# Attention and a capacity-routed mixture of experts on one core: five routing searches end after ten rounds, their count products get a later place, and the last 64 rows of an expert become one piece of the schedule

## The chip, the core and the metric

The kernel runs on one core of a Trainium2 chip. The metric is the time of the whole kernel on the device in microseconds (us), the median of several runs. TensorE (PE in the profile) multiplies matrices; PEld is its weight load. VectorE (DVE), ScalarE (ACT) and GpSimd (POOL) work on elements; SyncE (SP) starts transfers. Each engine takes its instructions strictly in the order in which the program lists them. An instruction that waits therefore holds everything behind it on its engine.

## The reference

Attention over 8 batches, 8 heads, 576 positions and 64 values, with a causal mask by blocks of 64, gives 4608 rows of 512 values. Each row goes to exactly one of 8 experts, and each expert takes exactly 576 rows:

```python
logits = x @ w_gate                       # 4608 x 8
order = np.argsort(-logits.flatten())
for idx in order:                         # from the largest logit down
    tok, e = idx // E, idx % E
    if assigned[tok] >= 0 or counts[e] >= cap: continue
    assigned[tok] = e; counts[e] += 1     # cap = 576
for e in range(E):
    mask = assigned == e
    out[mask] = np.maximum(x[mask] @ w1[e], 0) @ w2[e]   # 512 -> 1024 -> 512
```

Which expert fills first, and with which rows, depends on the data, so the kernel has to find it out on the chip.

## The kernel before

**Attention** takes the first half of the span and is not touched. It leaves the rows in DRAM (`x`) and the logits on the chip (`L`).

**The expert part** fills experts one after another. Step k (0 to 7) finds the expert that fills next, its 576 rows, and then computes them. `route(k)` is the search. Each row that is still free proposes to its best remaining expert (L740, L756, L758), and for all 8 experts at once the kernel looks for the value above which exactly 576 proposals lie. It does so in rounds. A round divides the interval in four: three candidates are written (L795, VectorE), two of them are counted on VectorE (L803, `jk`), the third on ScalarE (L772, `ja`, a sum of signs), a small product on TensorE adds the counts over the partitions (L819, `tot`, the count product), and VectorE turns the totals into the next step (L822, `sg`). After round t the interval is 4 to the power of minus t in the units of the search, so 14 rounds (`NS=14`) resolve the numbers fully. In round 6 (`NSC=6`) ScalarE also writes a shifted copy of the proposals (L776), with which the later, finer rounds work. `finish` (L898) then takes the highest threshold of the 8 experts (`heads`, L825), `place` and `invert` turn the rows found into a list of indices with three groups of small products (L963 to L967, `po`; L1065, `pe`; L1072, `ps`), and POOL gathers the rows by that list (L1140).

Step 0 and step 1 are different. Step 0 has four rounds and a guess that it checks. Step 1 has eight rounds (`EX={1:8}`) and then `early` (L874): one more pass on VectorE counts the proposals below the threshold found so far (L879), a product adds them up (L883, `wn`), and three short operations (L887 to L890) form a flag that is non-zero only when a single expert has the highest threshold and exactly 576 proposals lie above it. VectorE loads the flag into a register and branches (L892 to L896): where the flag is zero, `general` (L849) runs the rounds that were left out, on VectorE alone; otherwise it is skipped. Step 7 needs no search, since one expert is left.

`ffn(k)` computes an expert's 576 rows. The first product (L1191, `h`) has two halves of 256 and 320 rows with eight groups of 12 matmuls each; each group is taken out of its PSUM bank by ScalarE (L1177, `HH`) and VectorE (L1179, `HL`). Four banks carry the tag `g`. The second product (`y`) has five parts: m = 0 to 3 with 128 rows (L1217, eight pieces of three matmuls), and m = 4 with the last 64 rows (L1221, four pieces of six matmuls, which use half the columns of the array at a time, in pairs). The weights of an expert come in 8 transfers (`raw`), which ScalarE splits in halves (L1102, L1106) and POOL subtracts (L1109). POOL may start on them only when the next search has begun (`began`, L700, and the gate of L1108), and there are six `raw` buffers.

**The order of the work** is written by a planner, `Sched`, when the program is built. Each task is a Python generator that yields the engine, the cost in ns and the events that it needs, and then emits the instructions of one piece. The planner keeps a planned time for each engine and picks the task that can start first, a task of a better priority (lower number) before others; the order that comes out is fixed in the program. A search has priority 0, its count product too; `ffn` has priority 3. `lag(t)` moves the planned readiness of a task's next piece back by t ns. It emits nothing: it only changes where the planner puts the piece among those of its engine. The next search (k) is let in when the second product of expert k-2 begins (event `mid`). Planned costs that matter here are 645 ns for a piece of L1217 and 720 ns for a piece of L1221.

## Time and profile before

| what | us |
| --- | --- |
| median of three runs | 772.76 (770.9 to 775.21) |
| the profiled execution's own time | 774.55 |
| its span (first to last instruction) | 772.1 |
| PE busy | 712.9 (92%) |
| DVE busy | 554.8 (72%) |
| ACT busy | 533.0 (69%) |
| POOL busy | 467.2 (61%) |

The profile is one execution. Its time lies 2.45 us above its span, and 1.79 us above the median of the runs. Rows of the timeline read: start, duration, engine, line and operation, what it writes and reads, shapes, count; in brackets how long the engine was idle before it, and what ended the wait. Steps are told apart by time: the second products of experts 1, 2, 3 and 4 begin near 444, 495, 546 and 597 us, and the searches for experts 3, 4, 5 and 6 with them.

### The profile page before, as it was taken

To read this page: it belongs to the slowest core of one execution; us is meant where nothing else is said; L and a number is where in the kernel's file an instruction comes from. 1 tells how busy PE (TensorE), PEld (TensorE's weight loads), DVE (VectorE), ACT (ScalarE), POOL (GpSimd) and SP (SyncE) were. 2 spreads that over 40 slices of the span, in tenths; PEclk is the share of its full clock that TensorE was granted. 3 is DMA by queue.
4 is the path that set the end of the run, shared out by engine and by line. 5 is a ranking of instruction groups with operands and counts; after the bars stand their busy time and mean duration, and the time that the engine had idled before them with its cause. 6 is when DMAs were issued, how large, how long until landed. Compare 5 with 4: busy or idle time off the path is not lost.

```text
span 772.1 us, 18932 instructions
## 1 busy us (share of the span) xinstructions
PE 712.9 (92%) x6493; PEld 473.3 (61%) x6493; DVE 554.8 (72%) x2260; ACT 533.0 (69%) x1438; POOL 467.2 (61%) x520
## 2 busy tenths in 40 slices
PE   5889999999999999966999989999999999999997
PEld 3556676766776777743545736547557475574753
DVE  6899889998799878768897968579587693420210
ACT  5788888988898898844755696774865848383211
POOL 5888878997799876613431485480762825766001
PEclk9999999999999999987999999999999999999999
DMA  9888999999999994256267291933915719862101
GB/s 203 164 157 171 204 188 213 205 166 226 191 203 179 215 211 85 78 124 209 81 183 214 91 284 37 276 107 100 260 65 207 162 38 268 276 164 62 35 14 48
DMA packets 249122, 122.83 MB, mean 159 GB/s; under 512 B 205600, under 2 KB 232096, under 8 KB 249024
## 3 DMA queue, kind: packets, MB, share of 16 engines
q1 hardware_dynamic: 243088, 102.60, 59.7%
q0 software_dynamic: 5936, 19.01, 7.5%
q8 instruction: 51, 0.84, 0.4%
q14 instruction: 47, 0.39, 0.2%
HBM read 71.45 MB, written 18.87 MB: 117 GB/s over the span
## 4 chain that ended last, share of the span: by engine, by line
PE 37%; DVE 5%; ACT 4%; DMA 4%; issue 2%; POOL 1%; another core or an unknown queue 0%; POOLq 0%; SPq 0%; DVEq 0%; ACTq 0%
PE y L1217 18%; PE h L1191 16%; PE y L1221 2%; DMA out_dram<-yo,ix 2%; ACT W L1106 1%; ACT raw L1102 1%; DMA raw<-in_moe_w_dram 1%; DVE jk L803 1%; DVE HL L1179 1%; POOL xg L1140 1%; DVE cd L795 1%; DMA xg<-x,ix 1%; PE pe L1065 1%; ACT ja L772 0%; ACT HH L1177 0%
## 5 line engine op out<-in xcount | busy, mean ns | idle before, releaser
L442 POOL TENSOR_TENSOR P<-P,m 128x320 f32<-128x320 f32 (+8 forms) x285 | 209.4, 771 | 45.9 <-DVE m L434 30.6
L1191 PE MATMUL h<-X,W 128*128 128x320 f16 (+3 forms) x1536 | 194.9, 286 | 1.0 <-DVE HL L1179 0.5
L1191 PEld LDWEIGHTS <-W 128*128 128x128 f16 x1536 | 142.5, 98 | 45.5 <-issue 4.8
L420 ACT ACTIVATE P<-psb,m 128x576 f32<-128x576 f32 (+8 forms) x288 | 149.7, 548 | 25.6 <-DVE m L413 17.8
L1217 PE MATMUL y<-W,HH 128*128 128x512 f16 x512 | 152.2, 379 | 0.0
L409 DVE TENSOR_REDUCE m<-psb 128x1 f32<-128x576 f32 (+8 forms) x288 | 124.7, 479 | 10.8 <-PE psb L384 10.5
L1109 POOL TENSOR_TENSOR W<-raw,W 128x1024 f16<-128x1024 f32 x56 | 118.1, 2135 | 14.4 <-ACT W L1106 12.8
L467 PE MATMUL psb<-mident,P 128*128 128x128 f32 x800 | 104.5, 278 | 11.1 <-POOL P L442 5.1
L384 PEld LDWEIGHTS <-qT 128*64 128x64 f16 x1408 | 77.1, 111 | 42.3 <-issue 28.1
L1177 ACT ACTIVATE HH<-h 128x320 f16<-128x320 f32 (+3 forms) x128 | 51.8, 409 | 71.6 <-PE h L1191 64.0
L1207 POOL DMA_INDIRECT out_dram<-yo,ix x40 | 39.0, 975 | 102.6 <-ACT yo L1199 65.5
L384 PE MATMUL psb<-kT,qT 128*64 128x288 f16 (+8 forms) x704 | 90.8, 284 | 10.8 <-ACT P L420 9.6
L467 PEld LDWEIGHTS psb<-mident,P 128*128 128x128 f32 x800 | 86.3, 141 | 22.6 <-POOL P L442 7.0
L1140 POOL DMA_INDIRECT xg<-x,ix x40 | 40.9, 1023 | 96.5 <-DVE ix L1074 51.5
L502 PE MATMUL psb<-PT,V 128*64 128x448 f32 (+5 forms) x776 | 97.2, 388 | 0.9 <-DVE PT L450 0.4
L1179 DVE SCALAR_TENSOR_TENSOR HL<-h,HH 128x320 f16<-128x320 f32 (+3 forms) x128 | 57.2, 452 | 55.8 <-ACT HH L1177 47.7
L1217 PE MATMUL y<-W,HL 128*128 128x512 f16 x256 | 97.0, 379 | 0.0
L448 ACT ACTIVATE PT<-psb 128x512 f32<-128x512 f32 (+1 forms) x165 | 82.6, 596 | 6.0 <-PE psb L467 5.7
L384 PE MATMUL psb<-kS,qT 128*64 128x288 f16 (+8 forms) x704 | 83.2, 281 | 0.4 <-DVE kS L354 0.2
L1217 PEld LDWEIGHTS <-HH 128*128 128x128 f16 x512 | 46.9, 97 | 50.2 <-issue 0.4
L1102 ACT ACTIVATE raw<-raw 128x512 f32<-128x512 f32 x112 | 67.9, 625 | 8.4 <-DMA raw<-in_moe_w_dram 8.2
L502 PEld LDWEIGHTS psb<-PT,V 128*64 128x64 f32 x776 | 49.5, 137 | 32.2 <-issue 24.3
(251 smaller groups left out, 1018.5 us busy)
## 6 DMA issues: line engine op xcount, KB each, us to landing
raw<-in_moe_w_dram SPq DMA_DIRECT2D x64, 512.0 KB
x<-XR SPq DMA_DIRECT2D x8, 1152.0 KB
kn<-in_k_dram SPq DMA_DIRECT2D x15, 576.0 KB
qn<-in_q_dram SPq DMA_DIRECT2D x15, 576.0 KB
V<-in_v_dram SPq DMA_DIRECT2D x64, 128.0 KB
V<-in_v_dram SPq DMA_DIRECT2D x16, 64.0 KB
xg<-x,ix POOLq DMA_INDIRECT x41
out_dram<-yo,ix POOLq DMA_INDIRECT x40
```

Source lines behind the costliest of these rows:

```text
L384: nc.tensor.matmul(out if len(K1.shape) == 2 else out.rearrange("p (r j) -> p r j", r=2), lhsT=A[:, h, 64 * i:64 * i + 64], rhs=K1, start= ...
L409: nc.vector.tensor_reduce(m[:, 0, c:c + 1], ps[:, o:o + 64 * (i + 1)] if g else s.part(ps, g, i, o), axis=AX.X if g else AX.XY, op=OP.max)
L420: nc.scalar.activation(out, in_, AF.Exp, bias=m[:, 1, c:c + 1], scale=s.ESC, accum_out=m[:, 2, c:c + 1])
L442: nc.gpsimd.tensor_tensor(sl, sl, m[:, 3, c:c + 1].to_broadcast([P, w]), op=OP.mult)
L448: s.nc.scalar.activation(out, in_, AF.Copy)
L467: nc.tensor.transpose(ps[:, a], s.Pb[n % s.NP][:, s.OFF[i] + 128 * j:s.OFF[i] + 128 * j + P], s.ident)
L502: nc.tensor.matmul(ps[64 * h:64 * h + 64, 64 * (i0 - b0):64 * (b1 - b0)], lhsT=vn[:, j, 2 * (n % 2) + h, :], rhs=pt[:, s.PTI[(j, i0)]:s.PT ...
L1102: nc.scalar.activation(raw[:,x],raw[:,x],AF.Copy,scale=s.WS)
L1109: nc.gpsimd.tensor_tensor(lw,raw,hi,op=OP.subtract)
L1179: nc.vector.scalar_tensor_tensor(HL[:,f,ts],ps,0.0,HH[:,f,ts],op0=OP.max,op1=OP.subtract)
L1191: nc.tensor.matmul(ps,lhsT=W[:,a,d,f*P:f*P+P],rhs=X[:,4*(d//2)+d%2+l,ts],start=(d==0 and n==0),stop=(d==3 and n==2))
L1217: if m<4: nc.tensor.matmul(ps,lhsT=Z[:,f,m*P:m*P+P],rhs=Y[:,a,f],start=(f==n==0),stop=(f==7 and n==2))
```

## The change

Three edits:

1. `EX` gets the steps 2 to 6 with ten rounds each. These searches now run rounds 0 to 9, leave out the shifted copy of round 6, and go through `early` with its extra pass, product, flag and branch. The body that is skipped holds four rounds.
2. After the passes of a round of a search k > 1 the planner is told to place the count product later: 800 ns in the first round, 300 ns in the others.
3. For k > 0 the part m = 4 of the second product is one piece of 2880 planned ns. The same 24 matmuls come out in the same order; the planner can no longer put another task between them.

```diff
-        s.NS=14; s.NSC=6; s.NX=4; s.EX={1:8}
+        s.NS=14; s.NSC=6; s.NX=4; s.EX={1:8,2:10,3:10,4:10,5:10,6:10}
...
                     if live: sc.busy(D,330 if k==0 else 150)
+                    if live and k>1: sc.lag(300 if t else 800)
                     yield T,30,('sg',k,t)
                     tot=s.ps.tile([P,512],F32,tag="tot",name=f"tot{k}_{t}")
                     nc.tensor.matmul(tot[:,0:3],lhsT=s.bo,rhs=cnt,start=True,stop=True)
...
             for f in range(8 if m<4 else 4):
-                yield T,645 if m<4 else 720,*[(x,k,y) for g in ((f,) if m<4 else (f,f+4)) for x,y in (('h',g),('h',8+g),('wc',4+g//2))],'g' if f==0 else None
+                wf=[(x,k,y) for g in ((f,) if m<4 else (f,f+4) if k==0 else range(8)) for x,y in (('h',g),('h',8+g),('wc',4+g//2))]
+                if m<4 or k==0 or f==0: yield T,645 if m<4 else 720 if k==0 else 2880,*wf,'g' if f==0 else None
                 if f==0: gk=sc.gtake(); ps=s.ps.tile([P,512],F32,tag="g",name=f"y{k}_{m}",bufs=4)
```

## The prediction

> **What bounds the kernel now.** I read the page first, then the busy time by stage of the expert part, then the waits, then the timeline around each wait of TensorE.

> ```profile
> PE 712.9 (92%) x6493; PEld 473.3 (61%) x6493; DVE 554.8 (72%) x2260; ACT 533.0 (69%) x1438; POOL 467.2 (61%) x520
> ...
> q8 instruction: 51, 0.84, 0.4%
> ```

> PE is busy for 92%, so shorter work elsewhere counts only where it lets PE stop waiting. The view of stages (start and end, length, busy time of PE, PEld, DVE, ACT, POOL) cut at the first matmul of experts 1 to 7 shows how much that is:

> ```profile
> 416.26:470.36 54.10, 50.06 (x381) 30.64 (x380) 43.12 (x230) 43.25 (x104) 34.49 (x24) 1.00 0.51 160
> 470.36:521.12 50.76, 49.55 (x378) 30.33 (x376) 38.14 (x206) 34.83 (x84) 28.17 (x20) 1.00 0.51 154
> 521.12:571.97 50.85, 49.63 (x379) 30.42 (x377) 38.20 (x206) 34.80 (x84) 26.55 (x19) 1.00 0.57 154
> 571.97:622.90 50.93, 49.54 (x379) 30.38 (x377) 38.09 (x206) 34.58 (x84) 26.55 (x19) 1.00 0.55 153
> 622.90:671.67 48.77, 48.77 (x370) 30.16 (x368) 28.29 (x108) 28.01 (x61) 26.78 (x19) 1.00 0.75 213
> 671.67:719.93 48.26, 48.26 (x358) 30.03 (x356) 8.28 (x19) 25.16 (x53) 27.32 (x19) 1.00 0.41 109
> ```

> Expert 6, beside which no search runs, takes 48.26 us without a gap, at a granted clock of 1.00. Experts 1 to 5 take 5.84, 2.50, 2.59, 2.67 and 0.51 us more: 14.1 us, the most that this change could return. Who stops PE from 416 to 672 us is said by its waits:

> ```profile
> PE tot L819 <- ACT ja L772: 5.1, 4, 1.4
> PE tot L819 <- DVE jk L803: 2.1, 1, 2.1
> PE po L964 <- DVE MM L920: 0.6, 1, 0.6
> ```

> Five count products hold PE for 7.2 us. Each is placed in PE's order at a point that PE reaches before the counts are there. One of the five, and what its neighbours do (PE, then ACT, then DVE), and the four others:

> ```profile
> 550.18 0.38 PE L1217 MATMUL y<-W,HL 128*128 128x512 f16 x1
> 551.77 0.16 PE L819 MATMUL tot<-cn,m_bo 128*128 128x3 f16 x1 [1.21 <-ACT ja L772]
> ...
> 554.16 0.38 PE L1217 MATMUL y<-W,HL 128*128 128x512 f16 x1
> 554.38 0.17 PE L819 MATMUL tot<-cn,m_bo 128*128 128x3 f16 x1
> 554.41 0.59 PE L1217 MATMUL y<-W,HH 128*128 128x512 f16 x2
> ```

> ```profile
> 548.38 0.44 ACT L1177 ACTIVATE HH<-h 128x320 f16<-128x320 f32 x1 [0.95 <-remote]
> ...
> 551.06 0.56 ACT L772 ACTIVATE ja<-m_PB,bs 128x324 f16<-128x324 f32 x1
> ```

> ```profile
> 551.55 0.08 DVE L803 DVE_READ_ACCUMULATOR jk<-m_PB,bs 128x1 f16 x1
> ```

> ```profile
> 419.64 0.16 PE L819 MATMUL tot<-cn,m_bo 128*128 128x3 f16 x1 [1.25 <-ACT ja L772]
> ...
> 454.21 0.18 PE L819 MATMUL tot<-cn,m_bo 128*128 128x3 f16 x1 [2.12 <-DVE jk L803]
> ...
> 501.00 0.16 PE L819 MATMUL tot<-cn,m_bo 128*128 128x3 f16 x1 [1.21 <-ACT ja L772]
> ...
> 602.79 0.16 PE L819 MATMUL tot<-cn,m_bo 128*128 128x3 f16 x1 [1.39 <-ACT ja L772]
> ```

> The rows at 501.00, 551.77 and 602.79 are the first rounds of the searches for experts 4, 5 and 6: ACT is late, because the weights' conversions fill its queue and one `HH` waited 0.95 us, so `ja`, and DVE's passes, end only near 551.6. The two at 419.64 and 454.21 lie inside the searches for experts 2 and 3.

> **The change part by part.**

> *Ten rounds and a test.* Four rounds go from each of five searches, so 20 count products leave PE's order. One costs PE 554.41 - 554.16 = 0.25 us against 0.215 for a matmul of L1217 (half of the 0.43 between neighbours): 0.035 us, so 0.7 us. What the test adds is seen once, in the search for expert 1:

> ```profile
> 381.19 0.51 DVE L879 TENSOR_SCALAR_CACHE_REDUCE jx<-m_PB,CB 128x288 f16<-128x288 f32 x1
> ...
> 385.16 0.17 DVE L890 SCALAR_TENSOR_TENSOR x<-wn,x 128x8 f32<-128x8 f32 x1
> ...
> 386.51 0.19 DVE L908 TENSOR_TENSOR sm<-m_BC,f 128x32 f32<-128x32 f32 x1 [1.17 <-DVEq L896]
> ```

> ```profile
> 382.23 0.17 PE L883 MATMUL wn<-m_bo,cx 128*128 128x8 f16 x1
> 382.26 7.54 PE L1191 MATMUL h<-X,W 128*128 128x448 f16 x39
> ```

> That is some 0.5 us of pass, 0.6 us of short operations (about three at 0.2 us) and 1.17 us in which DVE loads and branches: 2.3 us on DVE per search, against four rounds of about 2 us. Behind the branch on DVE stand the `HL` that free PSUM banks. In the row at 382.26 PE runs 39 matmuls without a gap through the whole of it, so it is covered; the product `wn` costs PE 0.035 us if its pass is ready, five times, and up to a DVE pass of 0.5 us each if not. I take 0.1 us each, 0.5 us, nearer the row.

> The search is not what the experts wait for, but it moves other work:

> ```profile
> 528.60 0.10 PEld L819 LDWEIGHTS <-m_bo 128*128 128x128 f16 x1 [0.28 <-DVE jk L803]
> ```

> ```profile
> 533.08 0.14 DVE L917 CAST eidx<-m 128x1 int32<-128x1 f32 x1
> ...
> 549.46 0.06 DVE L700 MEMSET gate<- 128x1 f32 x1
> ```

> ```profile
> 534.69 5.87 DMA raw<-in_moe_w_dram
> ```

> The search for expert 4 runs its 14 products from 501.00 to 528.60, 27.6/13 = 2.12 us a round. Ten end near 501.0 + 9 x 2.12 = 520.1, and with the m = 4 part in the way near 521; the test adds 2.3, so `eidx` comes at about 528.5 instead of 533.1. The weights' eight transfers on SP's queue and the five gathers on POOL's start some 4.5 us sooner. Both queues are free for it: X is needed only at 571.97. ACT can convert six pieces (six `raw` buffers; POOL frees none before the gate at 549.46), so its backlog before the first round of the next search should end some 4 us sooner too. That is a second reason for the stalls at 501, 551 and 602 to shrink, beside the lag.

> *The lag.* It adds no instruction. A piece of L1217 is 0.645 us (three matmuls). 800 ns puts one piece, or two, ahead of the first count product; what PE does in the wait is then work. So each of the three stalls (1.21, 1.21, 1.39 idle; 1.37, 1.37 and 1.55 us with the rest of the pitch, since 551.77 - 550.18 - 0.215 = 1.37) loses between 0 (ACT later by as much) and all. One piece alone would return 0.645; with the earlier conversions I take 1.2 each, 3.6 us. What becomes late is the first round, by no more than now, as PE waits for that product already. 300 ns in the other rounds is less than half a piece: a round of three pieces (1.94 us) mostly stays one. For the stalls at 419.64 and 454.21 (with the same 0.16 more, 1.41 and 2.28 us) the ends are 0 and the whole. The second has an odd cause:

> ```profile
> 452.54 0.16 DVE L822 SCALAR_TENSOR_TENSOR sg<-tot,m_wk 128x3 f32<-128x3 f32 x1 [2.65 <-PE y L1217]
> ```

> ```profile
> 449.96 0.17 PE L819 MATMUL tot<-cn,m_bo 128*128 128x3 f16 x1
> ```

> ```profile
> 450.16 0.92 POOL L1140 DMA_INDIRECT xg<-x,ix  x1 [0.30 <-issue]
> ```

> DVE got word of a product of 449.96 only at 452.5, while POOL was gathering. The gathers of expert 2 move ahead, so I take 1.3 of the 2.28; of the 1.41 I take 0.5. In the first product (h) the last products of a search wait a little (0.28 before the weight load at 528.60) and go with their rounds: 0.1 a search, 0.5 us in all, between 0 and 1.4.

> *The last 64 rows as one piece.* Today a count product falls inside L1221 in experts 1 to 4:

> ```profile
> 518.18 0.62 PE L1221 MATMUL y<-W,HH 128*64 128x512 f16 x4
> ...
> 520.25 0.18 PE L819 MATMUL tot<-cn,m_bo 128*128 128x3 f16 x1
> ...
> 521.12 1.16 PE L1191 MATMUL h<-X,W 128*128 128x256 f16 x9
> ```

> ```profile
> 668.96 0.62 PE L1221 MATMUL y<-W,HH 128*64 128x512 f16 x4
> ...
> 671.67 1.59 PE L1191 MATMUL h<-X,W 128*128 128x256 f16 x13
> ```

> 2.94 us with it, 2.71 without: 0.23 each, 0.9 us. Its cost is that a count product can wait 2.7 us behind the block, which the search can afford.

> *Sum:* 0.7 - 0.5 + 3.6 + 1.3 + 0.5 + 0.5 + 0.9 = 7.0 us. Against the profiled execution's 774.55 that gives 767.5; the median lies 1.8 lower, so **765.8 us**. The bounds: with no stall gone 0.7 - 2.5 + 0.9, about a loss of 1 (five `wn` at 0.5); with every named stall gone 8.0 + 0.6 (`po`) + 0.7 + 1.4 + 0.9 - 0.2, 11.4 gained.

> **The rivals.**

> *The stalls only move.* The new order is planned with the same costs, and what they miss (an `HH` that waits 0.95, a product heard of 2 us late) stays. For: these delays recur in each expert. Against: they meet a product that is now placed later. Only the sure terms are left, 0.7 - 0.1 + 0.9 = 1.5: 771.3 us.

> *All of the excess goes.* Of the 14.1 us, 50 remaining products keep 1.8 and the other small products about 1: 11 us, 761.8 on the scale of the median. Against: waits such as `po` have nothing to do with the lag.

> *The branch holds DVE too long* (slower). [...] If the target had to be fetched when the branch is taken, the hold is no more 1.17 but up to 1.17 + 5.87, the longest landing above, with the weights' transfers in the same engines. PE has four banks; a group of 12 matmuls of 256 is 1.3 us, so three groups, 3.9 us, less some 1.3 for `HH` and `HL`: PE starves once the hold passes 2.6 us. At the most that is 4.4 us each, five times 22, less the 7.0: 788 us; it makes the whole slower from 1.4 us each. Against: in the one branch seen the hold is 1.17, with a longer body to skip.

> [...]

> *The test fails* and `general` runs: four rounds on DVE alone, each three passes of 0.51 with their candidates and about 17 short operations of 0.17, near 5 us, so 20 us; less the cover 17 per search: 783 us for one. I worked out the thresholds from the reference's own inputs: in steps 2 to 6 the gap between the 576th and the 577th proposal is at least 8.0e-6 of the search's unit, over twice the 3.8e-6 that ten rounds resolve, and no two experts tie. So the test should pass.

> **How the numbers follow.** Chances: forecast 0.61 (own range 762 to 769), stalls only move 0.26, all goes 0.06, branch 0.05, test 0.02. A measurement of this kernel tells 0.5%, 3.9 us, from no change: faster is below 768.9, slower above 776.6. Faster gets most of the forecast, all of the third case and a little of the second, 0.64; the rest of these is the same, 0.28; slower 0.08, the last two and a little of the second. The range of 761 to 773 leaves out the two slow cases and the tails.

> **What would show it.** Right: the first count products after 501, 551 and 602 no longer have idle time of over 0.7 us before them; experts 2 to 4 take about 49 us from first matmul to first matmul; no L819 between L1221; the gathers start some 4 us earlier within an expert; five gaps of about 1.2 us behind L896 with PE busy through them. Wrong: the same gaps under other names, such as the product `wn`, `po` or `HL`, stages still near 50.5, or a hold at the branch of over 2.6 us.

## The result and the profile after

The change made the kernel slower: 775.44 us against 772.12, medians of 20 runs each (772.79 to 780.11 and 768.6 to 775.25). The ratio over the runs is 1.0053, with a 95% interval of 1.0039 to 1.0068 (the quotient of the two medians is 1.0043). The forecast was 765.8 us, and the range ended at 773.

The profiled execution of after took 778.35 us, that of before 774.55. Each lies above its median, by 2.9 and 2.4 us, so the two can be laid side by side. In after, lines below L816 have numbers that are one to two higher (L842 of before is L843, L1191 is L1192, L1221 is L1223).

From the page of after, the span and the busy time of each engine:

```profile
span 776.5 us, 18680 instructions
...
PE 714.0 (92%) x6478; PEld 475.3 (61%) x6478; DVE 534.0 (69%) x2085; ACT 519.3 (67%) x1393; POOL 466.5 (60%) x520
```

DVE lost 20.8 us of work and ACT 13.7, and PE has 15 instructions fewer: 20 count products less five `wn`. The work was taken out as planned. The stages of after, cut at the first matmul of experts 1 to 7 as before (start and end, length, busy time of PE, PEld, DVE, ACT, POOL, granted clock):

```profile
416.83:477.86 61.03, 52.12 (x376) 31.62 (x375) 42.27 (x175) 40.05 (x92) 35.86 (x24) 0.94 0.49 137
477.86:528.02 50.16, 49.23 (x377) 30.69 (x376) 32.48 (x169) 31.82 (x74) 27.02 (x20) 1.00 0.58 160
528.02:577.19 49.17, 49.05 (x376) 30.66 (x375) 32.49 (x169) 31.90 (x74) 26.05 (x19) 1.00 0.58 158
577.19:627.49 50.30, 49.22 (x376) 30.66 (x375) 32.53 (x169) 31.82 (x74) 27.14 (x20) 1.00 0.59 155
627.49:676.06 48.57, 48.57 (x369) 30.15 (x367) 26.55 (x98) 27.14 (x57) 25.79 (x19) 1.00 0.75 209
```

Expert 1 took 61.03 us instead of 54.10: 6.9 us more. Experts 2 to 6 took 246.48 instead of 249.57: 3.1 less (expert 6 is 48.28 in after). The start of expert 1 came 0.6 us later, and the rest after 724.34 is 52.2 us in both. Together 4.4 us of span. So the loss stands in one stage, and its idle time went from 4.04 to 8.91 us while PE's busy time rose by 2.06. What PE waited for in after, 416 to 677 us:

```profile
PE h L1192 <- DVE HL L1180: 6.2, 1, 6.2
PE tot L820 <- ACT ja L772: 4.6, 5, 2.1
```

One wait of 6.2 us is new. DVE around it (columns: start, duration, engine, line, operation):

```profile
428.10 8.79 DVE L843 SCALAR_TENSOR_TENSOR f<-th,m,m_wt 128x8 f32<-128x8 f32 x1
...
437.29 0.42 DVE L1180 SCALAR_TENSOR_TENSOR HL<-h,HH 128x256 f16<-128x256 f32 x1
...
439.54 0.19 DVE L909 TENSOR_TENSOR sm<-m_BC,f 128x32 f32<-128x32 f32 x1 [1.15 <-DVEq L897]
```

POOL in the same stretch:

```profile
427.58 0.91 POOL L1208 DMA_INDIRECT out_dram<-yo,ix  x1 [2.79 <-DVE CB L881]
428.51 8.36 POOL L1110 TENSOR_TENSOR W<-raw,W 128x1024 f16<-128x1024 f32 x4
```

And PE:

```profile
427.19 4.41 PE L1192 MATMUL h<-X,W 128*128 128x256 f16 x36
437.76 5.48 PE L1192 MATMUL h<-X,W 128*128 128x320 f16 x21 [6.17 <-DVE HL L1180]
```

An operation on 8 elements per partition, which takes 0.23 us elsewhere, took 8.79. It is one of the first operations of `heads` in the search for expert 2. It began 0.41 us before the row of POOL's run of four conversions of expert 1's weights and ended when that run ended (436.87). The next `HL` stood behind it on DVE, PE's four banks filled, and PE stopped. The branch (1.15 us of idle time before L909) came only after that and stopped nothing.

The pause had a second price. The view of busy time by stretches, PE's clock in the third column from the end:

```profile
437.76:442.46 4.70, 4.70 (x18) 2.60 (x18) 3.41 (x20) 0.44 (x1) 0.00 (x0) 0.50 0.01 2
442.46:447.00 4.54, 4.54 (x36) 3.23 (x35) 4.37 (x17) 1.50 (x3) 0.00 (x0) 0.96 0.72 235
```

For 4.7 us after the pause PE was granted half its clock. It did 18 matmuls there; at the pitch of the matmuls that follow (33 in 4.64 us, 0.14 each) they take 2.5 us. So the hold cost 6.2 + 2.2 = 8.4 us.

In before the same work met less of the run. DVE, then POOL:

```profile
432.82 0.23 DVE L842 SCALAR_TENSOR_TENSOR f<-th,m,m_wt 128x8 f32<-128x8 f32 x1
...
433.58 1.71 DVE L848 TENSOR_SCALAR f<-f,m 128x8 f32<-128x8 f32 x1
```

```profile
426.49 6.32 POOL L1109 TENSOR_TENSOR W<-raw,W 128x1024 f16<-128x1024 f32 x3
433.14 2.13 POOL L1109 TENSOR_TENSOR W<-raw,W 128x1024 f16<-128x1024 f32 x1 [0.33 <-ACT W L1106]
```

The head came at 432.8, 4.7 us later; L842 fell in POOL's pause of 0.33 us and only L848 was held, to 435.3, when the last conversion ended. POOL's run itself came 2.0 us later (426.5 before, 428.5 after). With four rounds less the head of that one search stands at the beginning of the run instead of near its end.

The second thing that the profile of after shows is why experts 2 to 4 gained less than hoped. Rows of the chain of waits:

```profile
561.11 4.99 DMA raw<-in_moe_w_dram
...
566.18 0.63 ACT raw L1103
...
567.85 0.56 ACT ja L772 x2
...
568.45 0.16 PE tot L820
...
574.51 2.71 PE y L1223 x24
```

SP's queue in that stretch:

```profile
552.71 6.17 SPq L1167 DMA_TRANSPOSE X<-xg  x3
559.13 0.39 SPq L1079 DMA_DIRECT2D raw<-in_moe_w_dram  x1
559.62 1.23 SPq L1167 DMA_TRANSPOSE X<-xg  x1
561.11 0.37 SPq L1079 DMA_DIRECT2D raw<-in_moe_w_dram  x1
```

The seventh and the eighth transfer of an expert's weights stand on SP's queue behind the transposes of X. They were issued behind them, the last landed at 566.1, the conversion that ScalarE had next in its order waited for it, `ja` stood behind the conversion, and a count product of round 3 or 4 waited for `ja`. In after such gaps of 0.26 to 0.98 us, with 0.16 of the pitch in each, stand before the count products at 466.9, 469.8, 515.7, 519.3, 568.4, 615.4 and 618.7: 3.9 us in all. ScalarE's wait for the weights, 470 to 640 us, in after:

```profile
ACT raw L1103 <- DMA raw<-in_moe_w_dram: 6.6, 7, 2.3
```

and in before:

```profile
ACT raw L1102 <- DMA raw<-in_moe_w_dram: 2.9, 4, 1.5
```

### The profile page after: what moved, and what is told of

Read it like the earlier page. It is cut to its first block, busy times and chain, and to the rows that moved or that the text cites. A ratio compares the mean times of both kernels' runs of the same rounds, so it can differ in the third digit from the quotient of the medians.

```text
span 776.5 us, 18680 instructions
## 1 busy us (share of the span) xinstructions
PE 714.0 (92%) x6478; PEld 475.3 (61%) x6478; DVE 534.0 (69%) x2085; ACT 519.3 (67%) x1393; POOL 466.5 (60%) x520
## 5 line engine op out<-in xcount | busy, mean ns | idle before, releaser
L1192 PE MATMUL h<-X,W 128*128 128x320 f16 (+3 forms) x1536 | 196.9, 288 | 7.0 <-DVE HL L1180 6.5
L1192 PEld LDWEIGHTS <-W 128*128 128x128 f16 x1536 | 143.8, 98 | 50.8 <-issue 8.7
L384 PE MATMUL psb<-kT,qT 128*64 128x288 f16 (+8 forms) x704 | 90.4, 283 | 11.5 <-ACT P L420 9.9
L502 PEld LDWEIGHTS psb<-PT,V 128*64 128x64 f32 x776 | 49.4, 137 | 32.3 <-issue 24.4
```

What stands on the lines that cost most here:

```text
L384: nc.tensor.matmul(out if len(K1.shape) == 2 else out.rearrange("p (r j) -> p r j", r=2), lhsT=A[:, h, 64 * i:64 * i + 64], rhs=K1, start= ...
L502: nc.tensor.matmul(ps[64 * h:64 * h + 64, 64 * (i0 - b0):64 * (b1 - b0)], lhsT=vn[:, j, 2 * (n % 2) + h, :], rhs=pt[:, s.PTI[(j, i0)]:s.PT ...
L1192: nc.tensor.matmul(ps,lhsT=W[:,a,d,f*P:f*P+P],rhs=X[:,4*(d//2)+d%2+l,ts],start=(d==0 and n==0),stop=(d==3 and n==2))
```

## The experiments

The theory to be tested (P in the expectations, where it has a letter): POOL's run of conversions holds DVE's short operations, DVE's `HL` behind them are late, and this one place costs more than the rest of the change gives. Its rivals: the new order by itself makes the loss through count products that wait (no POOL in it), or the ten rounds with their test cost it at the branch. Each ratio is to before on the same chip, with its 95% interval. Lengths of the stages, from the first matmul of an expert to that of the next, in the one profile of each kernel:

| kernel | 1 | 2 | 3 | 4 | ratio |
| --- | --- | --- | --- | --- | --- |
| before | 54.10 | 50.76 | 50.85 | 50.93 | 1 |
| before, second profile | 52.96 | 49.40 | 50.13 | 50.02 | |
| after | 61.03 | 50.16 | 49.17 | 50.30 | 1.0053 |
| ten rounds only | 57.81 | 49.32 | 49.11 | 49.31 | 1.0029 |
| lag only | 49.18 | 49.83 | 49.16 | 49.22 | 0.9935 |
| block only | 51.71 | 51.34 | 52.53 | 51.82 | 1.0049 |
| lag, ten rounds in steps 3 to 6 only | 51.60 | 49.89 | 51.14 | 51.41 | 0.993 |
| ten rounds, and conversions on DVE | 50.85 | 49.56 | 49.11 | 49.30 | 0.9926 |
| lag, and conversions on DVE | 51.78 | 50.06 | 50.71 | 50.61 | 1.001 |
| after, step 2 with 14 rounds | 49.48 | 49.26 | 49.67 | 50.52 | 0.9924 |
| after, conversions on DVE | 49.71 | 50.24 | 50.84 | 50.01 | 0.9897 |
| after, POOL writes zeros | 53.33 | 50.36 | 50.01 | 50.05 | |
| after, twice the work on POOL | 60.93 | 49.98 | 49.98 | 50.64 | |
| after, stops on POOL | 56.98 | 48.90 | 49.24 | 50.17 | |
| after, landings planned later | 58.82 | 48.90 | 48.90 | 48.89 | 1.0007 |
| the same, and step 2 with 14 rounds | 49.88 | 48.92 | 48.89 | 48.90 | 0.9889 |
| the same, and conversions on DVE | 50.10 | 48.90 | 48.89 | 48.90 | 0.992 |

**Each edit alone.** First the ten rounds on before:

```diff
-        s.NS=14; s.NSC=6; s.NX=4; s.EX={1:8}
+        s.NS=14; s.NSC=6; s.NX=4; s.EX={1:8,2:10,3:10,4:10,5:10,6:10}
```

> The kernel before with the ten rounds and the test in steps 2 to 6 alone: no lag, the last 64 rows in four pieces. Theory P (one VectorE operation at the head of search 2 stands behind POOL's run of four conversions, 8.8 us in the changed kernel, and TensorE loses 6.2 us to it): the operation of line 842 in search 2 again takes 6 to 9 us, expert 1 takes 58 to 61 us from first to first matmul, and the time is 774 to 779 us. Rival B (the five branches cost, about 1.3 us each): no long operation is needed, each of experts 1 to 5 is 1 us longer, 777 us. Rival L (the later place of the count products costs): without the lag nothing is lost, 768 to 771 us.

774.43 us, 1.0029 (1.0007 to 1.0052). Its waits of PE from 416 to 677 us have one row:

```profile
PE h L1191 <- DVE HL L1179: 6.5, 1, 6.5
```

DVE in its profile, then POOL:

```profile
426.35 8.21 DVE L908 TENSOR_TENSOR sm<-m_BC,f 128x32 f32<-128x32 f32 x1 [1.16 <-DVEq L896]
```

```profile
426.14 8.36 POOL L1109 TENSOR_TENSOR W<-raw,W 128x1024 f16<-128x1024 f32 x4
```

Another operation is the victim, 32 elements per partition behind the branch, and it too lasts to the end of POOL's run (434.5). The hold goes with the ten rounds, without lag or block. Its experts 2 to 4 have no wait of PE at all.

Then the lag on before:

```diff
+                    if live and k>1: sc.lag(300 if t else 800)
```

> The kernel before with the later place of the count products alone, 14 rounds and no test in steps 2 to 6. Theory P: the head of search 2 comes no earlier than before, so no VectorE operation near it takes over 2 us; some of the waits at the first count products go, 767 to 772 us. Rival B: the same, since there are no branches. Rival L: the search gets longer and expert 2 or its successors wait, 774 to 778 us.

766.33 us, 0.9935 (0.9908 to 0.9961). The head of search 2 stays late (434.1, its L843 takes 0.49 us), and PE waits once, 0.3 us. The gain of 5.0 us is near what the forecast gave the lag (3.6, 1.3 and 0.5), but more of it lies in the stage of expert 1 than the 1.8 us forecast there: this stage takes 49.18 us against 54.10 and 52.96 in the two profiles of before, the next three together 148.2 against 152.5 and 149.6.

Then the block on before (the two lines of the change at the loop over f):

```diff
-                yield T,645 if m<4 else 720,*[...],'g' if f==0 else None
+                wf=[... (f,f+4) if k==0 else range(8) ...]
+                if m<4 or k==0 or f==0: yield T,645 if m<4 else 720 if k==0 else 2880,*wf,...
```

> The kernel before with the last 64 rows as one piece alone. All theories: no count product between the matmuls of that part, 0.23 us less in each of experts 1 to 4, 0.9 us in all; 771 us against 772, hardly to be told from no change.

776.48 us, 1.0049 (1.0026 to 1.0072): a loss where a gain of about 1 us was expected. PE's waits from 416 to 677 us:

```profile
PE tot L819 <- ACT ja L772: 6.0, 6, 2.3
PE tot L819 <- DVE jk L803: 1.0, 3, 0.3
```

The second row is the block's own: a count product set just ahead of the block waits 0.3 us three times. The first holds two waits of 2.3 and about 1.5 us (560.2 and 611.9) with the pattern of above, a `raw` landing behind the transposes: ScalarE's conversion at 558.47 had waited 3.29 us. Whether the block or the replanned order as a whole puts them there is not told apart.

**Search 2 left as it was.** After, with one entry taken out:

```diff
-        s.EX={1:8,2:10,3:10,4:10,5:10,6:10}
+        s.EX={1:8,3:10,4:10,5:10,6:10}
```

> The changed kernel with step 2 taken back to 14 rounds without the test (steps 3 to 6 keep ten). Theory P: no operation near the head of search 2 takes over 3 us, expert 1 falls from 61.0 to 53 to 56 us, and the time is 767 to 770 us, below the kernel before. Rival B: four of five branches stay, so only a fifth of the loss goes, 774 to 775 us. Rival L: all of the lag but for four rounds stays, 775 us.

766.8 us, 0.9924 (0.9893 to 0.9955); the stage of expert 1 takes 49.48 us. Ten rounds instead of 14 in this one search are worth 1.0053 - 0.9924 = 1.3%, 10 us, and the stage is 11.5 us shorter: 8.4 of the hold, 2.1 of the count product at 423.09, which does not wait now, and 1 of smaller things. POOL's run is the same in this kernel (426.83 to 435.6), only the head is late.

The same without the block (before with the lag, and ten rounds in steps 3 to 6):

```diff
-        s.EX={1:8}
+        s.EX={1:8,3:10,4:10,5:10,6:10}
...
+                    if live and k>1: sc.lag(300 if t else 800)
```

> The kernel before with the lag and with ten rounds and the test in steps 3 to 6 alone: step 2 keeps 14 rounds, and the last 64 rows stay four pieces. Theory: the two parts that gain without the block and without the meeting with POOL; experts 2 to 4 take 49.1 to 49.4 us as with the ten rounds alone, expert 1 49.2 as with the lag alone; 763 to 767 us. If the block is worth its 0.9 us of TensorE, it is that much slower than the kernel with the block (766.8 us).

771.62 us, 0.993 (0.9903 to 0.9956), on a chip where before takes 776.09. By its ratio it can't be told from the kernel with the block, so here the block neither gives nor costs time that this shows. The parts do not add up, though: stages of 49.1 to 49.4 us were expected, and its one profile has 49.89 to 51.60, with 5.8 us of waits before count products.

**The run taken off POOL.** After, with expert 1's four late conversions on DVE, as its first four are already:

```diff
-            if k<2 and n<4:
+            if k==1 or (k==0 and n<4):
```

> The changed kernel, but the second-product weights of expert 1 are subtracted by VectorE (as its first four pieces are already), not by POOL: POOL's run of four conversions beside the head of search 2 is gone, and VectorE has four operations of 1.2 us more. Theory P (VectorE waits for the whole run of POOL): no operation of the head takes over 1 us, TensorE's stall of 6.3 us near 438 us is gone, expert 1 takes 50 to 54 us instead of 61, the time is 766 to 770 us. Rival B (branch) and rival L (lag): 774 to 777 us, since neither is touched.

768.22 us, 0.9897 (0.9865 to 0.9928). The wait for `HL` is gone though DVE got 4 more operations of over 1 us; what PE still waits for:

```profile
PE tot L820 <- ACT ja L772: 3.7, 4, 1.2
PE tot L820 <- DVE jk L803: 0.6, 1, 0.6
```

The first-count stalls at 499.1, 549.2 and 599.9 (1.34, 1.22 and 1.10 us, with 0.16 of the pitch) stand in this kernel in spite of the lag. The head of search 2 now comes at 431.11, 1.7 us earlier than in before, and its L843 takes 0.22 us. Ten rounds and branch are all there, so they are not what costs.

**What in POOL's operation holds DVE.** For expert 1 POOL writes zeros instead of subtracting, so it reads nothing. (This leaves out the low halves of expert 1's second weights.)

```diff
-                nc.gpsimd.tensor_tensor(lw,raw,hi,op=OP.subtract)
+                if k==1: nc.gpsimd.memset(lw,0.0)
+                else: nc.gpsimd.tensor_tensor(lw,raw,hi,op=OP.subtract)
```

> The changed kernel in the same order of all instructions, but POOL writes zeros in place of expert 1's subtractions; this leaves out the low halves of that expert's second weights. POOL then only writes and reads nothing. Theory P in the form that VectorE's second operand waits for POOL's reads: the operation of line 843 in search 2 takes 0.2 to 0.3 us although POOL is at work, and TensorE's stall is gone, 767 to 771 us. Theory P in the form that any POOL work blocks: the operation lasts as long as the run of memsets, 3 to 5 us by an estimate of half the subtraction's time, the stall is 1 to 2 us. Rival B or L: 8.8 us and a stall of 6.3 as before.

One profile, 769.95 us, on a chip where before takes 776.09. DVE, then POOL:

```profile
425.42 4.10 DVE L844 COPY m_BC<-th 128x16 f32<-128x16 f32 x1
```

```profile
425.85 3.64 POOL L1110 MEMSET W<- 128x1024 f16 x4
```

L843, with its two inputs, ran in its usual time (425.28, 0.23 us); the next operation, a copy that takes 0.16 us in after, was held to the end of the four writes. L843 began 0.57 us before the first write's row. That lead is not what freed it: in the two kernels further down in which POOL subtracts, with the work doubled and with the landings planned later, L843 began 0.58 and 0.56 us before POOL's row and was held (2.75 and 8.95 us). So beside a POOL that reads and writes L843 is held (8.79 us in after), and beside one that only writes it goes free while the copy is held (0.23 and 4.10 us). Why the two operations differ is not shown.

Then twice the work on POOL, each subtraction of expert 1 done two times:

```diff
                 nc.gpsimd.tensor_tensor(lw,raw,hi,op=OP.subtract)
+                if k==1: nc.gpsimd.tensor_tensor(lw,raw,hi,op=OP.subtract)
```

> The changed kernel in the same order, but POOL does each of expert 1's four subtractions for the second product twice, 8 x 2.1 us in place of 4. Theory P: the operation of line 843 in search 2 lasts 17 us in place of 8.8 (to the end of the run), TensorE's stall grows from 6.3 to about 14.8 us, the time to 783 to 788 us. [...]

One profile, 778.59 us, on the chip where before takes 776.09, and a stage of expert 1 as long as in after (60.93 us). The expected single hold of 17 us did not come:

```profile
424.98 2.75 DVE L843 SCALAR_TENSOR_TENSOR f<-th,m,m_wt 128x8 f32<-128x8 f32 x1
...
427.99 1.94 DVE L849 TENSOR_SCALAR f<-f,m 128x8 f32<-128x8 f32 x1
...
430.42 1.59 DVE L889 TENSOR_SCALAR x<-f,x 128x8 f32<-128x8 f32 x1
```

```profile
425.56 2.14 POOL L1110 TENSOR_TENSOR W<-raw,W 128x1024 f16<-128x1024 f32 x1
427.77 2.12 POOL L1111 TENSOR_TENSOR W<-raw,W 128x1024 f16<-128x1024 f32 x1
429.86 2.13 POOL L1110 TENSOR_TENSOR W<-raw,W 128x1024 f16<-128x1024 f32 x1
```

DVE got through at the end of each POOL operation (427.7, 429.9, 432.0). The second subtraction writes where the first wrote; whether that is why is not shown. There were eight holds of 0.8 to 2.8 us, and PE was idle for 8.2 us in four gaps. So a hold does not simply grow with POOL's work. Between the two subtractions of a pair lies a stop of 0.07 us; between one pair and the next the trace shows none (429.89 and 429.86), and DVE got through there too, so a stop that can be seen is not the whole condition. The unchanged work with a stop behind each operation:

```diff
                 nc.gpsimd.tensor_tensor(lw,raw,hi,op=OP.subtract)
+                if k==1: nc.gpsimd.drain()
```

> The changed kernel, where POOL empties its pipeline (a drain) after each of expert 1's conversions. [...]

One profile, 773.57 us, on a chip where before takes 771.86. Three of the four rows of DVE that were held (the other is L915 at 434.44, 0.98 us):

```profile
426.72 2.62 DVE L843 SCALAR_TENSOR_TENSOR f<-th,m,m_wt 128x8 f32<-128x8 f32 x1
...
431.98 1.04 DVE L909 TENSOR_TENSOR sm<-m_BC,f 128x32 f32<-128x32 f32 x1 [1.15 <-DVEq L897]
...
436.01 1.74 DVE L921 TENSOR_TENSOR MM<-ge,MM 128x36 f16<-128x36 f16 x1
```

PE's waits of 6.2 us become one of 1.8 for `HL` and one of 2.6 for `po`. Four operations with stops of 1.55, 0.22 and 0.22 us between them hold DVE for 2.62 us at the most; without a stop 8.79. The stage of expert 1 is still 56.98 us.

**The other loss, the late landings.** After, with the planner told that the last two weights of experts 2 and up land 2.6 us later, the figure it already has for expert 1:

```diff
+                if k>1 and n>5: sc.ev['wl',k,n]+=2600
```

> The changed kernel, but the planner is told that the seventh and eighth weight transfer of experts 2 to 7 land 2.6 us later, so that it places their conversions later in ScalarE's order. Theory W (the count products near 519, 568, 615 and 619 us wait because a conversion that waits for one of these transfers stands ahead of the counting pass on ScalarE): ScalarE's waits for transfers fall from 6.6 us between 470 and 640 us to under 2, the stalls of 0.3 to 1.0 us at these products go, 2 to 3 us less: a ratio of 0.997 to 1.002 beside 1.005. If they come from somewhere else, nothing changes. The stall in expert 1 stays in either case.

772.48 us, 1.0007 (0.999 to 1.0024). Its stages of experts 1 to 3:

```profile
416.00:474.82 58.82, 51.60 (x376) 31.64 (x375) 42.40 (x175) 40.19 (x92) 35.65 (x24) 0.94 0.48 143
474.82:523.72 48.90, 48.90 (x376) 30.68 (x375) 32.47 (x169) 32.18 (x74) 26.70 (x20) 1.00 0.64 165
523.72:572.62 48.90, 48.90 (x377) 30.68 (x376) 32.48 (x169) 31.88 (x74) 26.52 (x19) 1.00 0.56 160
```

ScalarE's waits for these weights fall from 6.6 to 1.0 us (470 to 640 us). Experts 2 to 4 run without a gap, 2.9 us less than in after, and the ratio falls by 0.46%, 3.6 us. The hold stays (L843 takes 8.95 us, clock 0.94 in the stage), so this loss can be taken away without the other.

**How far one profile goes.** Before, once more:

> The kernel before, unchanged, for a second profile of it. It tells how much of a stage's length is this kernel's own scatter: if the waits of TensorE come from the fixed order, the stalls at the first count products of the searches for experts 4 to 6 stand again at 1.2 to 1.7 us each, and experts 2 to 4 take 50.4 to 51.2 us.

770.66 us. Its stages 2 to 4 are 49.40, 50.13 and 50.02, 3.0 us shorter together than in the first profile. The stalls did not come back: PE does not wait at all before the first counts of the searches for experts 4 to 6 (498.99, 548.37 and 598.50), where the first profile has 1.21 to 1.39 us, nor near 454. It waits 0.42 us at 419.29, and 0.60 and 0.50 before the fifth counts at 557.65 and 607.68. Here L842 took 3.19 us at 432.46: POOL's four conversions ran without the pause of 0.33 us (427.23 to 435.62), so the hold is there in before too, and its length hangs on some tenths of a us. It costs PE a wait there as well:

```profile
PE po L964 <- DVE MM L920: 2.0, 1, 2.0
```

In the first profile the hold is 1.5 us shorter (1.71) and so is this wait, 0.6 us: the row of `po` among the forecast's waits of PE was already the price of a hold.

**Combinations.** Ten rounds alone with the conversions on DVE:

```diff
-        s.EX={1:8}
+        s.EX={1:8,2:10,3:10,4:10,5:10,6:10}
...
-            if k<2 and n<4:
+            if k==1 or (k==0 and n<4):
```

> The kernel before with the ten rounds and the test in steps 2 to 6 and with expert 1's last four conversions on VectorE; no lag, no block. The ten rounds alone left no wait of TensorE for a count product in experts 2 to 4 (49.1 to 49.3 us each) and lost 6.6 us in expert 1. Theory P: without POOL beside the head of search 2 that loss goes, expert 1 takes 49 to 51 us, the ratio to the kernel before is 0.983 to 0.990. If the loss were the test's own (its branch or its pass), the ratio stays at 1.003.

765.4 us, 0.9926 (0.9905 to 0.9947): the second edit turns a loss of 0.3% into a gain of 0.7%, less than expected. The stage of expert 1 takes 50.85 us and keeps a wait of 1.4 us.

The lag alone with the conversions on DVE:

```diff
+                    if live and k>1: sc.lag(300 if t else 800)
...
-            if k<2 and n<4:
+            if k==1 or (k==0 and n<4):
```

> The kernel before with the lag and with expert 1's last four conversions on VectorE, 14 rounds. In the kernel with the lag alone the head of search 2 met POOL's run for 0.3 us only, so theory P leaves nothing to gain here: a ratio of 0.992 to 0.996, as with the lag alone (0.9935). A clear gain would mean that POOL's run costs expert 1 in some other way.

771.48 us, 1.001 (0.9984 to 1.0035). The gain of the lag (0.9935) is lost: count products wait 4.7 us in eight places. Here no hold was to be removed, and the new plan set the count products and ScalarE's conversions against each other anew. That a replanned order brings stalls of some us with it, whichever edit causes it, is the rival that kept its share.

Both losses met at once, first with the conversions on DVE, then with search 2 left at 14 rounds:

```diff
+                if k>1 and n>5: sc.ev['wl',k,n]+=2600
...
-            if k<2 and n<4:
+            if k==1 or (k==0 and n<4):
```

> The changed kernel with both causes taken away: transfers seven and eight planned 2.6 us later, and expert 1's last four conversions on VectorE. If the two causes are the whole difference: expert 1 takes 49 to 51 us, experts 2 to 4 48.9 us each, the stall of 6.3 us and those at the later count products are gone, and the ratio to the kernel before is 0.984 to 0.990 (the forecast was 0.991 to the median of before). If a third cause remains, the ratio stays above 0.993.

765.1 us, 0.992 (0.9891 to 0.9949). The stages are as expected (50.10 and three of 48.9) and PE waits once, 0.8 us; the ratio is a little above what was expected.

```diff
+                if k>1 and n>5: sc.ev['wl',k,n]+=2600
...
-        s.EX={1:8,2:10,3:10,4:10,5:10,6:10}
+        s.EX={1:8,3:10,4:10,5:10,6:10}
```

> The changed kernel with transfers seven and eight planned 2.6 us later and step 2 with 14 rounds and no test, so that its head comes after POOL's run. If the two causes are the whole difference: expert 1 takes 49 to 52 us, experts 2 to 4 about 48.9 us, ratio 0.984 to 0.991. The same third-cause mark: above 0.993.

763.31 us, 0.9889 (0.9866 to 0.9912). What PE waits for from 416 to 677 us:

```profile
PE tot L820 <- ACT ja L772: 0.6, 1, 0.6
```

This kernel beats before and after: 1.1% under before, and 1.6% under after by the two ratios. In the five pairs that take the hold away (ten rounds only, after twice, later landings twice) the ratio falls by 0.9 to 1.6%; with the lag alone, where there was none to take, moving the conversions raises it by 0.75%. So the hold is what these pairs have in common, and of each step a share can be the new order.

## Why the prediction was wrong, step by step

**The step that failed** is the one on moved work: "The search is not what the experts wait for, but it moves other work". It let the gathers and the transfers start some 4.5 us earlier and closed with "Both queues are free for it". Three things went otherwise. The search's own tail on DVE moves too, which was not asked; in search 2 it came 4.7 us earlier and met POOL's run, which is not gated for expert 1. In the later searches the work hardly moved, because a second step failed, "a round of three pieces (1.94 us) mostly stays one": with the lag a round takes four pieces (2.61 us), and ten rounds last nearly as long as the fourteen of before, 24.7 against 27.6 us from first to last product (17.9 with the ten rounds only). The search for expert 4 in after:

```profile
507.56 0.17 PE L820 MATMUL tot<-cn,m_bo 128*128 128x3 f16 x1
...
532.30 0.17 PE L820 MATMUL tot<-cn,m_bo 128*128 128x3 f16 x1
```

Its first gather comes 548.22 - 528.02 = 20.2 us into the stage of expert 3; before it was 541.15 - 521.12 = 20.0, with the ten rounds only 536.88 - 523.27 = 13.6. And SP's queue was not free for the seventh and eighth transfer: within the stage they start 1.6 us earlier, not 4.5.

The price of the meeting could have been worked out from before. POOL's run from 426.49 to 435.27 was there to read, and so were two operations of DVE that lasted far beyond their kind: the group of L848 has a mean of 477 ns over six, where one takes 0.23 us; and this one, normally 0.18 us, ended with POOL's last conversion at 668.95:

```profile
664.11 4.89 DVE L981 TENSOR_SCALAR h<-q 128x36 f16<-128x36 f32 x1
```

With the forecast's own 4.5 us, a head at 432.8 - 4.5 = 428.3 held to 435.3 is 7.0 us; less its cover of 2.6 that leaves PE idle for 4.4, and the sum of 7.0 falls to 2.6 even without the clock.

**Term by term.** *Fewer products, `wn`* (0.7 and -0.5): the instructions are gone and no `wn` waits; too small to be seen by itself. *First-count stalls* (3.6): the profile of after has none at the first counts, but the sum took them from one execution, and the second profile of before has none of the three either. Nor does the lag keep them away: the kernels with zeros and with twice the work on POOL, which keep the order of after, wait 0.92 to 1.19 us at these products. In after 3.9 us came before products of rounds 3 and 4 instead, so stages 2 to 4 averaged 49.9, not 49. *The stall at 454.21* (1.3) went, but the second profile of before lacks it too. *The one at 419.64* (0.5) is 0.42 us there; in after a product at 423.09 waits 2.13 us for a `ja` that stands behind three conversions on ScalarE. These three terms, 5.4 of the 7.0 us, were stalls of one execution. *The block* (0.9): 24 matmuls in 2.71 us with no count product among them, as forecast; but the kernel with the block alone is slower, and the one without it no worse, so the term gives nothing. *The tail of search 2*: no term, and 8.4 us.

**The rivals.** "The branch holds DVE too long" had the right consequence and the right cover: PE lost what the hold had beyond 8.79 - 6.17 = 2.6 us, as forecast (with the ten rounds alone 8.21 - 6.45 = 1.8, where the held operation stood further down the tail). PE stopped 3.5 us into the hold and went on 0.9 us after it. Its cause was wrong: the five holds at the branch are 0.83 to 1.17 us, and no run shows the 5.87 us that its sum adds for a fetch. "The stalls only move" holds in experts 2 to 4. The test never failed, and `general` did not run.

**What was right** shows when the hold is taken away: with search 2 at 14 rounds the same change gains 0.76%, 5.9 us, near the forecast of 7.0. That this comes so near is in part luck: the lag gains 5.0 us by itself, more of it in the stage of expert 1 than the 1.8 that the forecast had put there, and the stalls that it priced are not in every execution.

**Open:** how long the hold is in an average execution, since only profiled ones show it (8.79, 8.21 and 8.95 us in three kernels); what lets it pass from one POOL operation to the next; and why a plan with fewer stalls on paper gets others, as with the lag and the conversions on DVE.

## What to carry to other kernels

A step that ends earlier moves its own tail as well as what it starts: lay the new time of every instruction of the tail over the timelines of the other engines; here GpSimd's run of four subtractions (8.36 us) held VectorE for 8.79 us. Operations of VectorE far beyond the median of their kind (1.71 us against 0.23, 4.89 against 0.18), even once and even where nothing waits for them, were the sign of such runs in before, and the run's length, not the operation's, became the price once the head moved into it. Two edits can undo each other: the lag gave back in longer rounds most of what four rounds less had saved, so the plan of both together is the one to read. A stall of 1.3 us in one profile is not a term of a sum until a second profile has it too, and in an order written by a planner any edit deals the small stalls anew.

## What the runs showed of the hardware that was not expected

PE's clock fell to 0.50 in the pauses of 6.2 to 6.5 us and came back some 3 to 5 us after PE went on (3.2 us with the ten rounds only, 4.7 with the landings planned later, 5.1 in after, estimates from the clock of stretches of 1 us). The kernel with the stops on POOL had only pauses of 1.8 and 2.6 us, with 1.4 us of work between, and its clock fell to 0.50 for about 3.4 us all the same (438.5 to 441.5, with 0.85 and 0.73 in the half us before and after); a single gap of 2.12 us in before left it at 1.00 (450 to 460 us).
